# Column sums of V's weights moved from TensorE to DMA transposes and VectorE, V of four blocks from raw rows, and first loads in pairs

## The chip, the cores and the metric

The kernel runs on one core of a Trainium2 chip. The metric is the device time of one execution in microseconds, as the median of several runs. The kernel before took 237.02 us, the median of three runs from 236.8 to 237.28.

TensorE multiplies matrices and writes to PSUM, VectorE and ScalarE do element-wise work and copy PSUM to SBUF, GpSimd (POOL) does small work and issues some transfers, and SyncE (SP) issues most transfers. They run side by side and wait for each other through semaphores.

## The reference

The input x has 2048 rows of 512 numbers in bf16. Each row is layer-normalized once (`xn`). Two branches read `xn`, and their outputs are added to x:

```python
qkv = xn @ wqkv                       # 512 -> 3 x 512: 32 heads of 16
logits = q[s] . k[s - 2*w] * scale    # w = 0..7: eight rows back, two apart
o = sum_w softmax(logits)[w] * v[s - 2*w]
A = o @ wo                            # 512 -> 512

z = gelu(xn @ w_in)                   # 512 -> 1792, split into z1 and z2 of 896
g = w_sp @ layernorm(z2) + b_sp       # w_sp is 2048 x 2048, over the rows
B = (z1 * g) @ w_out                  # 896 -> 512
out = x + A + B
```

What matters here is V, the third part of `qkv`. Since the normalization is a subtraction and a scale per row, V can also be had from the raw rows: `v = rstd * (x @ wv) - rstd * mean * colsum(wv)`, where `colsum(wv)` is the sum of each of wv's 512 columns.

## The kernel before

The rows are cut into 16 blocks of 128. Every operation is recorded as a task with a name, an engine, an estimated duration, a priority, and the buffers that it reads and writes (`Plan.add`). A list scheduler (`Plan.schedule`) then simulates the engines with these estimates and fixes the order of tasks on each engine and the PSUM bank of each result; PSUM has eight banks of 512 fp32 columns, and some tasks need a pair. At run time each engine follows its list strictly and waits where a semaphore has not come. Besides, some orders are written out by hand (lines 1003 to 1015): for TensorE's first tasks, for VectorE's and ScalarE's first tasks. The table `land` (line 1018) tells the scheduler when the first loads are expected.

The stages in order of time:

- **Start.** TensorE runs eight matmuls on constants (`warm`, line 560) while the first loads come. ScalarE's queue issues blocks 0 and 1 of x, SP's queue the two halves of wv (256 KB each), block 2, the two halves of w_in's z2 part (448 KB each), blocks 3 to 7 one by one (128 KB each), Q's and K's weights, and blocks 8 to 15.
- **Layer norm** (`ln_block`): VectorE computes mean and variance (`bnst`, `bnag`, lines 599 and 601), POOL the power to -1/2 (`rstd`, line 611), VectorE the normalized block (`norm`, line 623). Blocks 0 to 3 are transposed by TensorE against an identity matrix (`xTr`, line 579) and copied to SBUF by ScalarE (`xTe`, line 587). Blocks 4 to 15 are transposed by DMA on SP's queue (`xTd`, line 617).
- **V of blocks 0 and 1** doesn't wait for the norm. The raw block is transposed (`xTx`, line 579) and copied (`xTc`, line 606), and V is computed from it (line 654). The column sums of wv come from TensorE, by four matmuls with a matrix of ones (`cs`, line 638); ScalarE copies them, negated, to `ncs` (line 642); VectorE adds mean times column sum in PSUM (`fix`, line 660); ScalarE scales by rstd, writes V in the order (d, h) (`Ve`, line 663), and POOL's queue stores it to `vscr` in DRAM (`Vw`, line 668). V of blocks 2 to 15 is computed from the normalized block.
- **z2** (`z2_block`, lines 766 to 779): 8 matmuls of 448 columns per block into a pair of banks, then GELU with row sums on ScalarE (`z2g`) and a square with row sums (`z2s`).
- **Q and K** (`qk_pair`, line 677) for waves of four blocks, into pairs of banks; VectorE forms the products for eight offsets (lines 698 and 703), TensorE reduces them over heads (`red`, line 713), and the softmax follows on VectorE and ScalarE (lines 728 to 752).
- **z1** (line 812), then the mixing over rows `g` (line 907), the longest stage, with w_sp transposed by DMA (line 880). Beside it VectorE multiplies the attention with V read back from DRAM (`ldVs`, `pv`, lines 930 to 941), and a DMA transposes the result (`OTd`, line 944).
- **Output** (lines 963 and 972): 11 matmuls per block, a final addition of x on VectorE (`fin`, line 978), and a store.

The lines of the hand-written order for TensorE and ScalarE that lie around the change:

```python
["xTx0", "cs_0", "V0_0", "xTx1", "cs_1", "V0_1", "xTr0", "V1_0", "xTr1", "V1_1",
 "z2_0_0", "z2_0_0b", "z2_0_1", "xTr2", "z2_1_0", "z2_1_1", "V2_0", "V2_1", "xTr3", "z2_2_0"]
("xTc0_0", "xTc0_1", "xTc1_0", "xTc1_1", "xTe0_0", "xTe0_2", "cse", "xTe1_0", "xTe2_0", "z2g0",
 "Ve0", "xTe3_0", "z2g1", "Ve1", "Ve2", "z2s0")
```

Of the kernel before, what the change touches and what calls it, by code (L numbers as in the profile page):

```python
# [36 lines left out]
class Plan:  # L37
# [85 lines left out]
    def schedule(self, dma_bw=300.0, xbar_bw=190.0, dma_lat=1300.0, dma_pre=400.0, issue=None, tol=40.0, land=None,  # L123
# [49 lines left out]
        while left:  # L173
            pick = None
            for e in ENGS:
                sc = []
                for t in cand[e]:
                    r = max(t.ready, free[e])
                    for b in t.banks:
                        if b.base is None:  # L180
                            p = place(b)
                            if p is None:
                                r = None
                                break
                            r = max(r, p[2])
# [31 lines left out]
            if t.dma is not None:  # L217
                iss = issue[e]
                t.eng_end = r + iss
# [4 lines left out]
                t.end = xe + dma_lat  # L224
# [114 lines left out]
def build_kernel(nc, A_x, A_wqkv, A_wo, B_x, B_w_in, B_w_sp, B_b_sp, B_w_out, out, report=False, emit=True):  # L339
# [12 lines left out]
    NWARM = 8  # L352
# [3 lines left out]
    vscr = nc.dram_tensor("vscr", (16 + S, 512), BF).ap()  # L356


    off = {}
# [11 lines left out]
    place(3584, w_in1=0, tg=0, On=2048, xcT=0, ncs=1024)  # L371
# [8 lines left out]
    off["xn"] = off["attn"]  # L380
    AR = top[0]
# [4 lines left out]
    for name, n in (("prime", 4), ("mx", 128), ("Zb", 256), ("Z", 128), ("maskt", 128), ("st6", NB * 6),  # L386
                    ("mv", NB * 2), ("vpe", NB), ("rstd", NB), ("s1", NB), ("s2", NB), ("m2", NB), ("msq", NB),
# [8 lines left out]
    with ExitStack() as es:  # L396
# [59 lines left out]
        for s_ in range(2):  # L456
            R1(("wv", s_), "wv", 1024, 1024 * s_)
# [8 lines left out]
        for hf in range(2):  # L466
            for b in range(2):
                R1(("xcT", b, hf), "xcT", 256, 512 * b + 256 * hf)
            R(("xnT", 0, hf), "sb", [(off["xnT"] + dc * S, off["xnT"] + dc * S + 128) for dc in (2 * hf, 2 * hf + 1)])
        R1("ncs", "ncs", 1024)  # L470
# [20 lines left out]
        def dma(eng, fn, nbytes, chan, reads=(), writes=(), name="", xbar=False, prio=0.0, after=()):  # L491
            return T(eng, fn, reads=reads, writes=writes, name=name, prio=prio, after=after,
                     dma=dict(chan=chan, nbytes=nbytes, xbar=xbar))
# [7 lines left out]
        ncs = A("ncs", 1024).bitcast(F32)  # L501
# [15 lines left out]
        def ld_wv(hf):  # L517
            dma("sp", lambda e: e.dma_start(AC(off["wv"] + 1024 * hf, [[512, 2], [1, 512]]),  # L518
                                            A_wqkv[256 * hf:256 * hf + 256, 1024:1536].rearrange("(c p) n -> p c n",
                                                                                               p=128)),  # L520
                256 * 512 * 2, ("wv", hf), writes=[("wv", hf)], name="ldwv%d" % hf)
# [13 lines left out]
        def ld_wqk(which, eng):  # L535
# [5 lines left out]
        dma("act", lambda e: e.dma_start(A("xin", 512), x2[0:128, :]), 128 * 512 * 2, ("xin", 0),  # L541
            writes=[("xin0", 0), ("xin0", 1)], name="ldx0")
        ld_x(1, "act")
        ld_wv(0)
        ld_wv(1)
        ld_x(2, "sp")
        ld_win2a()
        ld_win2b()
        ld_x(3, "sp")
        ld_x(4, "sp")  # L550
        ld_x(5, "sp")
        ld_x(6, "sp")
        ld_x(7, "sp")
# [19 lines left out]
        def pe_tr(src, keys, name):  # L573
# [8 lines left out]
            T("pe", tr, reads=keys + ["ident"], writes=[bk], est=(430.0 if name == "xTx0" else 4 * c_mm(128)), name=name)  # L582
# [10 lines left out]
        def ln_block(b):  # L593
# [9 lines left out]
            if b < 2:  # L603
                bc = pe_tr(xin, xk, "xTx%d" % b)
                for hf in range(2):
                    T("act", (lambda hf: lambda a: a.activation(A("xcT", 256, 512 * b + 256 * hf), P(bc, 256, 256 * hf),
                                                                ACTF.Copy))(hf),
                      reads=[bc], writes=[("xcT", b, hf)], est=c_act(256), name="xTc%d_%d" % (b, hf), prio=-1)
# [23 lines left out]
        def colsum():  # L632
            bk = plan.bank("cs")
            for hf in range(2):
                def mm(t, hf=hf):
                    last = None
                    for dc in (2 * hf, 2 * hf + 1):
                        last = t.matmul(P(bk, 512), ones[:, 0:128], A("wv", 512, 512 * dc), start=(dc == 0),
                                        stop=(dc == 3))
                    return last  # L640
                T("pe", mm, reads=[("wv", hf)], writes=[bk], est=2 * c_mm(512) * (1 if hf else 2), name="cs_%d" % hf, prio=2)
            T("act", lambda a: a.activation(ncs, P(bk, 512), ACTF.Copy, scale=-1.0), reads=[bk],  # L642
# [427 lines left out]
```

## Time and profile before

| | |
|---|---|
| median of three runs | 237.02 us |
| span of the profiled execution | 236.1 us |
| TensorE busy | 231.7 us (98%) |
| VectorE busy | 207.4 us (88%) |
| ScalarE busy | 96.5 us (41%) |
| moved by DMA | 43.86 MB, 186 GB/s over the span |

The profile is of one execution. Its span runs from the first to the last instruction, and the measured time holds some 0.9 us more around it. Times in the timeline are counted from the start of the span. PE is TensorE, PEld its weight loads, DVE VectorE, ACT ScalarE, SPq, ACTq and POOLq the queues of the engines that issue transfers. A line of the timeline gives start, length, engine, source line, operation, output and inputs, the count of instructions merged, and in brackets how long the engine had been idle and what ended that. Some matmul records are missing from the trace, so counts of matmuls in it are a little low.

### The profile page before, as it was taken

To read this page: it belongs to the slowest core of one execution; us is meant where nothing else is said; L and a number is where in the kernel's file an instruction comes from. 1 tells how busy PE (TensorE), PEld (TensorE's weight loads), DVE (VectorE), ACT (ScalarE), POOL (GpSimd) and SP (SyncE) were. 2 spreads that over 40 slices of the span, in tenths; PEclk is the share of its full clock that TensorE was granted. 3 is DMA by queue.
4 is the path that set the end of the run, shared out by engine and by line. 5 is a ranking of instruction groups with operands and counts; after the bars stand their busy time and mean duration, and the time that the engine had idled before them with its cause. 6 is when DMAs were issued, how large, how long until landed. Compare 5 with 4: busy or idle time off the path is not lost.

```text
span 236.1 us, 2974 instructions
## 1 busy us (share of the span) xinstructions
PE 231.7 (98%) x1114; PEld 109.1 (46%) x1135; DVE 207.4 (88%) x269; ACT 96.5 (41%) x145; POOL 32.7 (14%) x56
## 2 busy tenths in 40 slices
PE   8999999999999999999999999999999999999996
PEld 3455555555444444444444444444444444444443
DVE  3799899999998899999699998986989997999432
ACT  3598889888967895510120531111111111000000
POOL 2259650311733100000000000000000000000000
PEclk9999999999999999999999999999999999999999
DMA  7998969991048325430999999998995959936432
GB/s 211 352 283 163 243 146 217 195 202 44 22 165 260 92 85 69 104 118 0 226 347 252 225 266 180 200 304 187 346 258 175 261 161 303 193 95 181 135 96 69
DMA packets 82013, 43.86 MB, mean 186 GB/s; under 512 B 54336, under 2 KB 81360, under 8 KB 82000
## 3 DMA queue, kind: packets, MB, share of 16 engines
q1 hardware_dynamic: 80768, 41.27, 71.5%
q0 software_dynamic: 800, 2.11, 2.8%
q10 hardware_dynamic: 432, 0.30, 0.6%
q8 instruction: 9, 0.15, 0.3%
q14 instruction: 4, 0.03, 0.1%
HBM read 26.35 MB, written 4.21 MB: 129 GB/s over the span
## 4 chain that ended last, share of the span: by engine, by line
PE 94%; DMA 3%; SPq 1%; ACT 1%; issue 1%; DVE 0%
PE ps L907 41%; PE ps L677 12%; PE ps L972 10%; PE ps L812 10%; PE ps L766 9%; PE ps L963 6%; PE ps L654 5%; DMA arena<-in_B_w_in_dram 3%; PE ps L713 1%; ACT arena L774 0%; SPq L518 0%; ACT arena L587 0%; PE ps L579 0%; SPq L514 0%; SPq L524 0%
## 5 line engine op out<-in xcount | busy, mean ns | idle before, releaser
L907 PE MATMUL ps<-arena 128*128 128x512 bf16 x439 | 96.6, 379 | 0.5
L907 PEld LDWEIGHTS ps<-arena 128*128 128x128 bf16 x448 | 43.7, 98 | 53.1 <-issue 0.4
L915 ACT ACTIVATE arena<-ps 128x1024 bf16<-128x1024 f32 (+1 forms) x16 | 14.7, 917 | 78.0 <-PE ps L907 78.0
L698 DVE TENSOR_TENSOR arena<-arena 128x4096 bf16<-128x4096 bf16 x16 | 36.5, 2282 | 0.1
L935 DVE TENSOR_TENSOR arena<-arena 128x4096 bf16<-128x4096 bf16 x16 | 36.4, 2283 | 0.0
L938 DVE TENSOR_TENSOR arena<-arena 128x2048 bf16<-128x2048 bf16 (+1 forms) x32 | 29.9, 948 | 0.0
L677 PE MATMUL ps<-arena 128*128 128x512 bf16 x126 | 28.7, 379 | 0.1
L703 DVE TENSOR_TENSOR arena<-arena 128x4096 bf16<-128x4096 bf16 x12 | 27.4, 2287 | 0.1
L972 PE MATMUL ps<-arena 128*128 128x512 bf16 (+2 forms) x117 | 26.9, 366 | 0.1
L766 PE MATMUL ps<-arena 128*128 128x448 bf16 x128 | 26.0, 352 | 0.5 <-DMA arena<-in_B_w_in_dram 0.5
L812 PE MATMUL ps<-arena 128*128 128x512 bf16 x110 | 24.4, 379 | 0.1
L978 DVE TENSOR_TENSOR arena<-ps,arena 128x512 bf16<-128x512 f32 (+2 forms) x17 | 11.2, 658 | 11.7 <-PE ps L972 11.7
L677 PEld LDWEIGHTS ps<-arena 128*128 128x128 bf16 x128 | 14.5, 113 | 13.0
L766 PEld LDWEIGHTS ps<-arena 128*128 128x128 bf16 x128 | 12.3, 98 | 12.7 <-ACT arena L642 0.7
L686 ACT ACTIVATE arena<-ps 128x1024 bf16<-128x1024 f32 x16 | 16.3, 1021 | 4.4 <-PE ps L677 4.1
L972 PEld LDWEIGHTS ps<-arena 128*128 128x128 bf16 x119 | 11.4, 98 | 12.8
L812 PEld LDWEIGHTS ps<-arena 128*128 128x128 bf16 x112 | 10.9, 98 | 13.2 <-ACT arena L818 0.3
L963 PE MATMUL ps<-arena 128*128 128x512 bf16 (+2 forms) x66 | 16.5, 366 | 0.1
L774 ACT ACTIVATE arena<-ps 128x896 bf16<-128x896 f32 x16 | 14.6, 914 | 3.2 <-PE ps L766 3.1
L818 ACT ACTIVATE arena<-ps 128x1024 bf16<-128x1024 f32 (+1 forms) x16 | 13.9, 923 | 4.9 <-PE ps L812 4.8
L654 PE MATMUL ps<-arena 128*128 128x512 bf16 x60 | 15.6, 379 | 0.2
L779 ACT ACTIVATE arena<-arena 128x896 bf16<-128x896 bf16 x16 | 15.1, 945 | 0.0
(61 smaller groups left out, 168.5 us busy)
## 6 DMA issues: line engine op xcount, KB each, us to landing
arena<-vscr SPq DMA_DIRECT2D x16, 1024.0 KB, 7.1
arena<-in_A_x_dram SPq DMA_DIRECT2D x30, 128.0 KB, 3.6
vscr<-arena POOLq DMA_DIRECT2D x16, 128.0 KB, 3.0
out_dram<-arena SPq DMA_DIRECT2D x15, 128.0 KB, 1.8
arena<-in_A_wqkv_dram SPq DMA_DIRECT2D x2, 512.0 KB, 6.9
arena<-in_B_w_in_dram SPq DMA_DIRECT2D x2, 448.0 KB, 6.1
arena<-in_B_w_in_dram SPq DMA_DIRECT2D x1, 896.0 KB, 5.9
arena<-in_B_w_out_dram SPq DMA_DIRECT2D x1, 896.0 KB, 4.9
```

The costliest lines, as they stand in the source:

```text
L654: last = t.matmul(P(bk, 512), A("xcT", 128, 512 * b + 128 * dc) if b < 2 else xTv(b, dc), A("wv", 512, 512 * dc), start=(dc == 0), stop=(d ...
L677: last = t.matmul(P(bk, 512, 512 * which), AC(off["wqk"] + 2048 * which + 512 * dc + c, [[4, 128]]), AC(off["xnT"] + dc * S + 512 * j, [[1 ...
L686: T("act", lambda a: a.activation(AC(qo, [[ko - qo, 2], [1, 512]]), P(bk, 1024).rearrange("p (t n) -> p t n", t=2), ACTF.Copy, scale=0.5), ...
L698: T("dve", (lambda pbv, qb, kb: lambda v: v.tensor_tensor(pbv, qb, kb, ALU.mult))(pbv, qb, kb), reads=rd, writes=[("pb", s_)], est=c_tt(40 ...
L703: T("dve", (lambda av, bv: lambda v: v.tensor_tensor(av, av, bv, ALU.add))(av, bv), reads=[("pb", 1)], writes=[("pb", acc)], est=c_tt(4096 ...
L766: last = t.matmul(P(bk, 448, 512 * hf), xTv(b, dc), AC(off["w_in2"] + 896 * dc + 448 * hf, [[1, 448]]), start=(dc == 0), stop=(dc == 3))
L812: last = t.matmul(P(bk, 512, 512 * i), AC(off["w_in1"] + 896 * dc + 128 * fc, [[1, 128]]), AC(off["xnT"] + dc * S + 512 * j, [[1, 512]]), ...
L907: last = t.matmul(P(bk, 512, 512 * i), AC(off["z2"] + FH * sh + 128 * fc, [[1, 128]]), AC(off["wT%d" % r_] + sh * 512, [[1, 512]]), start= ...
L935: T("dve", lambda v: v.tensor_tensor(tv, tv, av, ALU.mult), reads=[("attn", b)], writes=[("Vs", sv)], est=c_tt(4096), name="pv%d" % b, pri ...
L938: T("dve", (lambda n: lambda v: v.tensor_tensor(A("Vs", n, 4096 * sv), A("Vs", n, 4096 * sv), A("Vs", n, 4096 * sv + n), ALU.add))(n), wri ...
L963: last = t.matmul(P(bk, cn), AC(off["OT"] + 512 * tb + 128 * cc, [[1, 128]]), AC(off["wo"] + 512 * cc + c0, [[1, cn]]), start=(cc == 0), s ...
L972: last = t.matmul(P(bk, cn), AC(off["z1T"] + fc * S + 128 * tb, [[1, 128]]), AC(off["w_out"] + 512 * fc + c0, [[1, cn]]), start=False, sto ...
```

## The change

1. **Column sums.** TensorE's four matmuls, ScalarE's copy and the buffer `ncs` go. Four DMA transposes on SP's queue (`wvT`) turn wv so that its columns lie along partitions; they are ordered after the transposes of blocks 4 to 11. One reduction on VectorE (`csum`) sums 2048 elements per partition to 4. The 512 sums are stored to DRAM by a transfer on POOL's queue (`csw`) and read back, broadcast to all partitions, by another (`csr`) into `csb`.
2. **V of blocks 0 to 3 from raw rows** (`NRAW = 4`). ScalarE copies each V out of PSUM with the factor rstd into an fp32 buffer (`vraw`); after the column sums are there, VectorE adds -mean * rstd (`mr`, one small operation for the four blocks) times column sum and writes V in the order (d, h) (`fix`). The store `Vw` follows. Blocks 2 and 3 get a raw transpose `xTx` and a copy `xTc`, and keep the normalized transpose, which z2, Q, K and z1 read. V's first matmuls are cut into finer tasks.
3. **Loads.** Block 0 comes as two halves of 64 partitions on SP's and ScalarE's queues. Blocks 2 and 3, 4 and 5, 6 and 7 come in pairs of 256 KB. The warm-up has seven matmuls.
4. **Orders and estimates.** The hand-written orders put V of blocks 0 to 3 ahead of z2; in ScalarE's order `xTe3` stands ahead of `z2g0`. The scheduler gets other estimates for DMA transposes and landings, and places two pairs of banks for one task at once. The buffers for raw transposes, `vraw`, `csb` and `wvT` lie in z1's area.

In the new fixed order, VectorE's column sum stands between its first and second wave-0 products, its four fixes ahead of wave 1's first product sum, and TensorE's first reduction `red0` behind z2 of block 15 and the first half of V of block 13.

```diff
+        for h, q_ in enumerate(("sp", "act")):
+            dma(q_, (lambda h: lambda e: e.dma_start(ar[64 * h:64 * h + 64, off["xin"]:off["xin"] + 512],
+                                                     x2[64 * h:64 * h + 64, :]))(h),
+                64 * 512 * 2, ("xin0", h), writes=[("xin0", h)], name="ldx0%s" % "ab"[h])
         ld_x(1, "act")
-        ld_wv(0)
-        ld_wv(1)
-        ld_x(2, "sp")
+        for d0, dn in ((0, 2), (2, 2)):
+            ld_wv(d0, dn)
+        ld_x2(2)
         ld_win2a()
         ld_win2b()
-        ld_x(3, "sp")
-        ld_x(4, "sp")
-        ld_x(5, "sp")
-        ld_x(6, "sp")
-        ld_x(7, "sp")
+        ld_x2(4)
+        ld_x2(6)
...
         def colsum():
-            bk = plan.bank("cs")
-            for hf in range(2):
-                def mm(t, hf=hf):
...
-                        last = t.matmul(P(bk, 512), ones[:, 0:128], A("wv", 512, 512 * dc), start=(dc == 0),
-                                        stop=(dc == 3))
...
-            T("act", lambda a: a.activation(ncs, P(bk, 512), ACTF.Copy, scale=-1.0), reads=[bk],
-              writes=["ncs"], est=c_act(512), name="cse", prio=-0.5)
+            for dc in range(4):
+                dma("sp", (lambda dc: lambda e: e.dma_start_transpose(AC(off["wvT"] + 128 * dc, [[512, 4], [1, 128]]),
+                                                                      A("wv", 512, 512 * dc)))(dc),
+                    128 * 512 * 2, ("wvT", dc), reads=[("wv", dc)], writes=[("wvT", dc)], name="wvT%d" % dc, xbar=True,
+                    prio=0.5, after=lnd[4:12])
+            T("dve", lambda v: v.tensor_reduce(Fv("cs", 4), AC(off["wvT"], [[512, 4], [1, 512]]), AX.X, ALU.add),
+              reads=[("wvT", dc) for dc in range(4)], writes=["cs"], est=2290, name="csum", prio=4.5)
+            dma("pool", lambda e: e.dma_start(bass.AP(tensor=cscr.tensor, offset=cscr.offset, ap=[[4, 128], [1, 4]]),
+                                              Fv("cs", 4)),
+                2048, "cswr", reads=["cs"], writes=["cscr"], name="csw", prio=1)
+            dma("pool", lambda e: e.dma_start(csb, bass.AP(tensor=cscr.tensor, offset=cscr.offset, ap=[[0, 128], [1, 512]])),
+                128 * 2048, "csrd", reads=["cscr"], writes=["csb"], name="csr", prio=1)
...
-            if b < 2:
-                T("dve", lambda v: v.scalar_tensor_tensor(P(bk, 512), ncs, Fv("mv", 1, 2 * b), P(bk, 512),
-                                                          ALU.mult, ALU.add),
-                  reads=["ncs", ("mv", b)], writes=[bk], est=690, name="fix%d" % b, prio=1)
...
+            if b < NRAW:
+                T("act", lambda a: a.activation(vraw(b), P(bk, 512), ACTF.Copy, scale=Fv("rstd", 1, b)),
+                  reads=[bk, ("rstd", b)], writes=[("vraw", b)], est=c_act(512), name="Ve%d" % b, prio=4)
+                T("dve", lambda v: v.scalar_tensor_tensor(
+                    vdh.rearrange("p d (c h) -> p d c h", c=4), csb.rearrange("p (h d c) -> p d c h", d=16, c=4), Fv("mr", 1, b),
+                    vraw(b).rearrange("p (c h d) -> p d c h", d=16, c=4), ALU.mult, ALU.add),
+                  reads=["csb", "mr", ("vraw", b)], writes=[("Vn", sl)], est=690, name="fix%d" % b, prio=6)
...
-                      ["xTx0", "cs_0", "V0_0", "xTx1", "cs_1", "V0_1", "xTr0", "V1_0", "xTr1", "V1_1",
-                       "z2_0_0", "z2_0_0b", "z2_0_1", "xTr2", "z2_1_0", "z2_1_1", "V2_0", "V2_1", "xTr3", "z2_2_0"],
+                      ["xTx0", "xTx1", "V0_0", "V0_1", "V1_0", "V1_1", "V0_2", "xTx2", "V0_3", "V1_2", "V1_3", "xTx3", "V2_0", "V2_2",
+                       "xTr0", "V3_0", "V3_2", "xTr1", "z2_0_0", "z2_0_0b", "z2_0_1", "xTr2", "z2_1_0", "z2_1_1", "xTr3", "z2_2_0"],
...
-                      ("xTc0_0", "xTc0_1", "xTc1_0", "xTc1_1", "xTe0_0", "xTe0_2", "cse", "xTe1_0", "xTe2_0", "z2g0",
-                       "Ve0", "xTe3_0", "z2g1", "Ve1", "Ve2", "z2s0"), ("V10_1", "Q3_3")):
+                      ("xTc0_0", "xTc0_1", "xTc1_0", "xTc1_1", "xTc2_0", "xTc3_0", "xTe0_0", "xTe0_2", "Ve0", "xTe1_0", "Ve1", "xTe2_0", "Ve2",
+                       "xTe3_0", "z2g0", "Ve3", "z2g1", "z2s0"), ("V10_2", "Q3_3")):
```

## The prediction

> **What bounds the kernel now.** I read the page's busy shares first, then the timeline of the first 22 us, the chain of work that ended last, and the landings of the first loads.
>
> ```profile
> span 236.1 us, 2974 instructions
> PE 231.7 (98%) x1114; PEld 109.1 (46%) x1135; DVE 207.4 (88%) x269; ACT 96.5 (41%) x145; POOL 32.7 (14%) x56
> ...
> PE 94%; DMA 3%; SPq 1%; ACT 1%; issue 1%; DVE 0%
> ```
>
> TensorE is on the chain for 94% of the span. The DMA share is one piece at the start, as the chain shows (start, length, what):
>
> ```profile
> 2.79 6.50 DMA arena<-in_B_w_in_dram
> 9.34 0.93 PE ps L766 x4
> ...
> 14.61 0.86 PE ps L654 x4
> 15.47 6.47 PE ps L677 x30
> ```
>
> The timeline puts the same stretch beside ScalarE:
>
> ```profile
> 0.84 2.93 PE L560 MATMUL ps<-const-bfloat16-1.0 128*128 128x512 bf16 x8 [0.84 <-PEq L1055]
> 3.73 0.61 PE L579 MATMUL ps<-arena 128*128 128x128 bf16 x4
> 4.26 0.85 PE L638 MATMUL ps<-arena,const-bfloat16-1.0 128*128 128x512 bf16 x2
> 4.38 0.66 ACT L606 ACTIVATE arena<-ps 128x256 bf16<-128x256 f32 x2 [1.14 <-PE ps L579]
> 4.95 0.60 PE L654 MATMUL ps<-arena 128*128 128x512 bf16 x2
> 8.22 0.92 PE L766 MATMUL ps<-arena 128*128 128x448 bf16 x4 [0.28 <-DMA arena<-in_B_w_in_dram]
> 9.34 0.93 PE L766 MATMUL ps<-arena 128*128 128x448 bf16 x4 [0.21 <-DMA arena<-in_B_w_in_dram]
> 12.71 0.39 PE L579 MATMUL ps<-arena 128*128 128x128 bf16 x4
> 13.13 0.60 ACT L587 ACTIVATE arena<-ps 128x512 bf16<-128x512 f32 x1 [0.53 <-PE ps L579]
> 13.63 0.91 ACT L774 ACTIVATE arena<-ps 128x896 bf16<-128x896 f32 x1
> 14.43 0.20 ACT L774 ACTIVATION_READ_ACCUMULATOR arena<-ps 128x1 f32 x1
> 15.31 6.64 PE L677 MATMUL ps<-arena 128*128 128x512 bf16 x30
> ```
>
> From 15.31, the first Q/K matmul, TensorE runs on to 234.2; the waits list none of its matmuls in that stretch. A 512-column matmul advances it by 0.216 us (the chain's 10.74 us for about 50 of them), a 448-column one by 0.189 (3.03 for 16), four 128-column ones by 0.22. Both versions have done the same work when Q/K starts, except for the column sum and two transposes. So **time after = time before − (15.31 − new start of Q/K) + any new wait behind it**, and I need only these two numbers. The profiled span of 236.1 lies 0.9 under the median of 237.02; I put differences on the median.
>
> **Before Q/K: the budget.** Between 3.73 and 15.31 TensorE does 4 column-sum, 16 V, 6 transpose groups (each like one 512 matmul) and 24 z2 matmuls: 26 × 0.216 + 24 × 0.189 = 10.15 us in 11.58. So 1.43 us is idle time or a slow clock (L638's two took 0.43 each, as in the warm-up; from 4.95 on the full rate shows). The change takes away 4 × 0.216 = 0.86 and adds the raw transposes of blocks 2 and 3, 0.43. The new floor is 3.51 + 24 × 0.216 + 24 × 0.189 = 13.2.
>
> **Where it will really start.** Step by step:
>
> 1. Warm-up: one 128-column matmul less, so it ends at 3.51 (2.93 less 0.107, from 0.84, with its tail) instead of 3.77. x0 landed at 3.7 (0.80 + 2.9). It now comes as two halves at the head of two queues, no longer beside a 256 KB weight load. Bounds 3.2 to 3.7; I take 3.55, so xTx0 starts there. *Against this:* the Trainium skill, "DMA: Bandwidth & Descriptors", Rules for kernel authors, says that two transfers to disjoint partition halves serialize on the same 16 engines and gain nothing; by it x0 lands at 3.7 again and the sum below would end at 236.65 instead of 236.5. No run here separates the two so far.
> 2. xTx0 to the first copied half took 0.65 (3.73 to 4.38), from there to the first V matmul 0.57. V0 starts at 4.77. wv's first half, now second on SP, lands between 4.2 (as before) and 4.65 (one issue of 0.45 later); not later than the copy.
> 3. V0_0, V0_1, V1_0, V1_1, V0_2 follow. The first pays 0.43, the others 0.216: 6.06 with no gap. x1 landed at 4.55, its transpose and copies let V1 start at 5.4 to 5.6, so up to 0.2 more. wv's second half landed at 5.3, in time. Then xTx2 needs the pair of blocks 2 and 3. Block 2 alone landed at 5.7; 131 KB more at the 350 GB/s of this stretch is 0.37, so 6.05. I take xTx2 at 6.15 (bounds 5.8 to 6.7, the upper if the pair is skewed as w_in's halves are).
> 4. From xTx2 to z2: 11 V matmuls and 4 transpose groups, 15 × 0.216 = 3.24, so z2 at 9.4.
> 5. The loads of w_in's second half have one more 128 KB ahead of them. They landed at 8.1 and 9.3 and were what TensorE waited for (0.28 and 0.21). Plus 0.37: 8.5 and 9.7, wanted at 9.4 and 10.15. This wait goes; what is late next is the V work put ahead of it.
> 6. z2 of blocks 0 to 2 and two transposes: 24 × 0.189 + 0.43 = 4.97, to 14.37.
> 7. A new wait: Q/K needs two banks, and ScalarE's written order puts the GELU of z2 block 0 (z2g0) behind xTe3, the copy of the last transpose. The rows for such a sequence: transposes start 12.71, GELU and its read-out end 14.63, 1.92 us, and 0.06 to be seen. TensorE has 0.22 + 1.51 to do meanwhile, so it idles 0.25. Q/K starts at 14.62.
>
> That is 0.69 earlier. Bounds: xTx2 at 5.8 gives 14.27 (1.04 earlier), at 6.7 gives 15.17 (0.14).
>
> **Behind Q/K: what moves and what covers it.**
>
> - SP: ten issues ahead of Q's and K's weights become eight, so these are not later than 12.7 and 14.2 where they landed. Four transposes of wv (1.27 us each on SP, from 10.48 for 8) go between the eighth and ninth xn transposes: 5.1 us, so blocks 12 to 15, issued by 31.2 before, land about 37 instead of 33.5; their first use, z2 of block 12, is at 49.2. The w_sp transposes behind them end by 56 instead of 50.9 and are wanted at 98.2.
> - VectorE: the column sum is 2048 elements in one reduce; L728's 1024 took 1.21, so 2.2 to 2.4. Fixes go from two to four, 0.75 each by L660; small `mr` 0.15. In all 2.3 + 1.5 + 0.15 = 3.95 us more, and the two early fixes (9.0 and 10.8) leave, so norms of blocks 4 to 7 come some 1.5 us sooner, which Q/K of wave 1 needs if it is to start 0.7 earlier.
> - The first logits reduction (L713, 64.64; VectorE had finished at 63.2) is the first place where TensorE meets that extra work. By the new order TensorE does z2 of block 15, V10 to V12, half of V13 and a Q/K pair ahead of it: about 6.25 us, so 64.64 + 6.25 − 0.69 = 70.2. VectorE does 2.3 + 3.0 + 0.15 and four z2 normalizations (1.8) more, and starts its products 1.5 to 2 earlier: 68.5 to 69. It holds by about 1.4 us.
> - Tail: the last transpose of the attention output is issued at 219.5, lands 3.3 later, and is wanted at 231.6. That is 8.8 us of slack against 3.95. VectorE's own idle time shows it, too:
>
> ```profile
> DVE arena L978 <- PE ps L972: 11.7, 10, 1.7
> ```
>
> - Column sums go out and come back by two transfers on POOL. Its 128 KB writes landed in 2.0 to 3.9 us, so twice that from 32 is 40; the fixes stand at about 53 in VectorE's order. Behind the first transfer on POOL stands the z2 power (3.05 us, L795), whose result VectorE uses 4.6 us later: covered by 0.8. V stores of blocks 0 to 3 move from 13.5-18.8 to after 54; V is read back from 97.7 on.
> - Output blocks: TensorE may wait once or twice for a bank behind VectorE's later final adds (0.69 each). Bounds 0 to 0.7; I take 0.15, since the final adds lag by up to 2.8 us now and eight banks hold 17 us of it.
>
> Sum: 237.02 − 0.69 + 0.15 = 236.5.
>
> **Rivals.**
>
> - *Cover that was there anyway* (B): the pair of x lands at 6.5 to 7, or ScalarE's longer queue (two copies of 0.6 more, the column sum's 0.6 less) delays a V copy. Q/K starts at 15.0 to 15.5: 236.7 to 237.2. For it: w_in's half took 2.4 us after x2 for its 459 KB, far under 350 GB/s. Against: each x row is a 1 KB piece, and x2 followed wv by 0.4.
> - *Slower: the clock rises late* (C). The full rate began at 4.95, after 4.1 us of nearly unbroken matmuls. The new order leaves TensorE idle around 3.95 to 4.77. If the rate then rises one stretch of that length later, matmuls from 4.95 cost double for some 3.4 us, 1.7 us lost less 0.2 of gaps: Q/K at 16.1, so 0.8 lost, and with the 0.15 for the output blocks 238.0. It decides if a V matmul after 6.0 still takes 0.43. The Trainium skill, "TensorE: Matmul & The Clock Gate", Part 1, states that an activity window of about 3.4 us, free-running, must be busy before the half rate is lifted, and gives no share that counts as busy. The rows agree with the half rate at first; the granted clock in the profile reads 1.00 throughout and doesn't show it.
> - *Slower: VectorE arrives late at the first reduction* (D). Its fixes now read 4-byte operands in a scattered order from SBUF. From 1.1 us each, or if the column sums return after 55, the 1.4 us of cover are gone and TensorE waits one for one. At 1.5 us each: 3.0 − 1.4 = 1.6 lost, 238.1. Against it: L730 reads PSUM scattered at 1.2 us for 1024, no dearer per element.
> - *More than forecast* (E): no waits at all, near the floor: 235.3 to 235.9.
>
> **How the numbers follow.** Forecast (A), Q/K at 14.3 to 15.0 and nothing lost behind: 236.0 to 236.7, 0.55. B 0.20, C 0.10, D 0.12, E 0.03. The likeliest gives 236.5. For 8 in 10 the range drops E, half of C and half of D: 235.9 to 238.0. A difference under 0.2% (0.47 us, 236.55 to 237.49) is about what can't be told from none: of A about 0.4 lies below 236.55 and 0.15 above, B gives 0.03 faster, 0.14 same, 0.03 slower, E is faster, C and D slower. That is 0.46, 0.29, 0.25.
>
> **What would show it.** Right: xTx2 at 6.0 to 6.3, z2's first matmul at 9.3 to 9.6 with no wait on w_in, Q/K's first at 14.6 behind a short wait for ScalarE L774, no TensorE wait over 0.1 us before the output blocks, VectorE's reduce 2.2 to 2.4, fixes near 0.75. Wrong: V matmuls of 0.43 past 6 us (C); a wait ahead of the 32-row reduction near 70 (D); xTx2 at 6.6 or later (B).

## The result, and the profile after

| | before | after |
|---|---|---|
| median | 236.91 us (6 runs, 236.78 to 237.37) | 238.99 us (6 runs, 237.81 to 239.72) |
| ratio after / before | | 1.0077, 95% interval 1.0056 to 1.0098 |
| span of the profiled execution | 236.1 us | 237.1 us |
| first Q/K matmul | 15.31 | 15.44 |
| from there to the end of the last matmul | 218.87 | 219.48 |
| from there to the end of the span | 1.92 | 2.18 |

The change made the kernel 2.1 us slower. It was forecast 0.5 us faster, and 238.99 lies above the range (235.9 to 238.0). The profiled execution took 238.31, so it is one of the quicker ones of the changed kernel. Its time exceeds its span by 1.2, and in the other executions below the two differ by 1.2 to 1.6; the prediction's 0.9 set the span of one execution against the median of others.

The busy times and the chain of the page, after:

```profile
span 237.1 us, 3018 instructions
PE 232.3 (98%) x1138; PEld 109.1 (46%) x1138; DVE 211.6 (89%) x273; ACT 96.9 (41%) x146; POOL 31.9 (13%) x58
...
PE 67%; DVE 22%; DMA 4%; SPq 3%; POOL 1%; issue 1%; DVEq 0%
```

TensorE fell from 94% of the chain to 67%, and VectorE holds 22% where it had none: somewhere TensorE now waits for VectorE. The timeline of the start shows another loss ahead of that (start, length, engine, line, operation, count; in brackets the idle time and what ended it):

```profile
0.80 0.59 SPq L566 DMA_DIRECT2D arena<-in_A_x_dram  x1
0.81 0.57 ACTq L566 DMA_DIRECT2D arena<-in_A_x_dram  x1
1.43 0.85 ACTq L534 DMA_DIRECT2D arena<-in_A_x_dram  x1
1.44 1.08 SPq L543 DMA_DIRECT2D arena<-in_A_wqkv_dram  x2
3.46 0.63 PE L602 MATMUL ps<-arena 128*128 128x128 bf16 x4
5.33 0.40 PE L602 MATMUL ps<-arena 128*128 128x128 bf16 x4 [1.24 <-DMA arena<-in_A_x_dram]
5.57 1.46 PE L692 MATMUL ps<-arena 128*128 128x512 bf16 x5
6.86 0.39 PE L602 MATMUL ps<-arena 128*128 128x128 bf16 x4
10.13 1.68 PE L806 MATMUL ps<-arena 128*128 128x448 bf16 x8
15.44 4.91 PE L717 MATMUL ps<-arena 128*128 128x512 bf16 x22 [0.16 <-ACT arena L814]
```

Block 0 did land early: its transpose starts at 3.46. Then TensorE stands still for 1.24 us, until block 1 lands at 5.33; it had landed at 4.55 before. From 5.33 on nothing holds it for longer than the 0.16 shown: 4.80 us from `xTx1` to z2 at 10.13, 5.3 more to Q/K.

The second loss is at the first logits reduction:

```profile
32.21 2.29 DVE L662 TENSOR_REDUCE fpool<-arena 128x4 f32<-128x2048 bf16 x1 [1.02 <-DMA arena<-arena]
54.06 4.19 DVE L701 SCALAR_TENSOR_TENSOR arena<-arena,fpool 128x512 bf16<-128x512 f32 x4
69.07 2.28 DVE L743 TENSOR_TENSOR arena<-arena 128x4096 bf16<-128x4096 bf16 x1
70.51 0.59 PE L692 MATMUL ps<-arena 128*128 128x512 bf16 x2
71.40 1.05 PE L753 MATMUL ps<-arena 128*32 128x512 bf16 x16 [0.29 <-DVE arena L743]
```

and in the waits of TensorE's weight loads (engine, line, what it waited for: us in total, times, longest):

```profile
PEld ps L753 <- DVE arena L743: 0.8, 1, 0.8
PEld ps L852 <- DVE arena L770: 0.6, 1, 0.6
```

The four fixes took 4.19 us instead of the 3.0 assumed. VectorE had also waited 1.02 for the transposes of wv. It finishes the sum that the reduction reads at 71.35 (69.07 + 2.28), after TensorE is ready for it. The 0.61 us that the stretch behind Q/K is longer lies here, by my estimate about 0.4 ahead of the reduction and 0.2 at the bank behind it (line 770).

So in this execution the span is 1.0 longer: 0.13 by Q/K, 0.61 behind it, and 0.26 after the last matmul. Against the forecast of 14.62, Q/K is 0.82 late. The rest of the median's 2.1 us had to be found in other executions; none at the median itself was profiled.

### The profile page after: what moved, and what is told of

It is laid out like the page before. It is cut to its first block, busy times and chain, and to the rows that moved or that the text cites. A ratio compares the mean times of both kernels' runs of the same rounds, so it can differ in the third digit from the quotient of the medians.

```text
span 237.1 us, 3018 instructions
## 1 busy us (share of the span) xinstructions
PE 232.3 (98%) x1138; PEld 109.1 (46%) x1138; DVE 211.6 (89%) x273; ACT 96.9 (41%) x146; POOL 31.9 (13%) x58
## 4 chain that ended last, share of the span: by engine, by line
PE 67%; DVE 22%; DMA 4%; SPq 3%; POOL 1%; issue 1%; DVEq 0%
PE ps L948 41%; PE ps L1013 10%; PE ps L852 10%; DVE arena L738 7%; PE ps L1004 6%; DVE arena L743 6%; DMA arena<-in_A_x_dram 3%; DVE arena L838 2%; SPq L658 2%; DVE arena L701 2%; DVE fpool L622 1%; DMA arena<-arena 1%; DVE arena L647 1%; DVE fpool L662 1%; POOL fpool L635 1%
## 5 line engine op out<-in xcount | busy, mean ns | idle before, releaser
L959 DVE TENSOR_TENSOR arena<-arena 128x1024 bf16<-128x1024 bf16 (+1 forms) x16 | 10.0, 625 | 5.8 <-ACT arena L956 5.8
```

## The experiments

Three explanations compete. **Loads:** the split of block 0 makes what is issued behind it late. **Clock:** TensorE's half rate lasts longer, or comes back, because TensorE is idle near 4 to 5 us. **VectorE:** the dear fixes make the first reduction late. Each run was timed beside runs of the kernel before on the same chip. "Behind Q/K" is the time from the first Q/K matmul to the end of the last matmul: 218.87 in both profiles of the kernel before.

### The changed kernel again

> The changed kernel once more, for the spread of its runs (237.8 to 239.7 so far) and a second profile. Theory F (VectorE's fixes at 1.1 us instead of 0.75 bring it late to the first logits reduction): Q/K again at about 15.4, a TensorE wait of 0.3 to 1.5 us ahead of the 32-row reduction near 71, and 0.2 to 0.6 for a bank behind it; the slow runs differ from the fast ones there. Rival S (the start): the profile shows the first transposes of x later or earlier by what the run is longer or shorter, with the wait at the reduction unchanged. Rival C (clock): V matmuls of 0.43 us past 6 us in a longer run.

Measured: 239.01 us (6 runs, 238.65 to 239.36), 1.0084 [1.0067, 1.0101]. The profiled execution took 238.65: Q/K at 16.02, 219.13 behind it.

```profile
5.32 1.04 PE L692 MATMUL ps<-arena 128*128 128x512 bf16 x4 [1.04 <-DMA arena<-in_A_wqkv_dram]
6.57 0.39 PE L692 MATMUL ps<-arena 128*128 128x512 bf16 x1 [0.20 <-DMA arena<-in_A_wqkv_dram]
7.22 0.40 PE L602 MATMUL ps<-arena 128*128 128x128 bf16 x4 [0.26 <-DMA arena<-in_A_x_dram]
```

This time block 1 was early and wv's first half late (issued at 1.44, landed at 5.24, against 4.2 before). The loss is the same in kind: what stands behind the halves of block 0 is late, on one queue or the other. Where ScalarE's queue took 0.85 us to issue block 1, as in the first profile, block 1 was late; here that issue took 0.59, SP's of wv's first half 0.82, and wv was late. The pair of blocks 2 and 3 is late here as well (7.2).

### Fixes that read in stored order

```diff
-                    vdh.rearrange("p d (c h) -> p d c h", c=4), csb.rearrange("p (h d c) -> p d c h", d=16, c=4), Fv("mr", 1, b),
-                    vraw(b).rearrange("p (c h d) -> p d c h", d=16, c=4), ALU.mult, ALU.add),
+                    vn, csb, Fv("mr", 1, b), vraw(b), ALU.mult, ALU.add),
```

> The four fixes read the scaled V and the column sums in stored order and write in stored order, all else the same, instruction for instruction; V of blocks 0 to 3 comes out in the wrong order of columns. Theory F: the fixes fall from 1.11 to about 0.7 us, VectorE is 1.6 us earlier at the first reduction, TensorE waits there no more, and the median falls by 0.7 to 1.5 us against the changed kernel. Rival S: fixes may be shorter, the median moves by under 0.3 us. If the scattered order isn't what costs, the fixes stay at 1.1.

This kernel leaves V of blocks 0 to 3 in the wrong order of columns. Measured: 239.38 us (6 runs, 237.60 to 240.23), 1.0094 [1.0063, 1.0124]. A fix took 746 ns. The groups by shape (busy us, mean ns of one | idle before), first of the changed kernel's second profile, then of this one:

```profile
L701 DVE SCALAR_TENSOR_TENSOR arena<-arena,fpool 128x512 bf16<-128x512 f32 x4 | 4.2, 1122 | 0.0
```

```profile
L701 DVE SCALAR_TENSOR_TENSOR arena<-arena,fpool 128x512 bf16<-128x512 f32 x4 | 2.7, 746 | 0.0
```

So the scattered order is what makes a fix dear. The wait at the reduction is gone and the stretch behind Q/K is back at 218.66, but this doesn't show that the cheap fixes removed it: TensorE itself came to the reduction 1.8 us later (73.21 instead of 71.40). VectorE was ready at 71.16; with dear fixes, some 1.5 us more, it would by that estimate still have been in time. The median didn't fall by the 0.7 to 1.5 that theory F asked for; the larger loss lies before Q/K, which began at 17.83 in this execution, the slowest of the six:

```profile
3.46 0.63 PE L602 MATMUL ps<-arena 128*128 128x128 bf16 x4
5.74 0.61 PE L602 MATMUL ps<-arena 128*128 128x128 bf16 x4 [1.65 <-DMA arena<-in_A_x_dram]
6.14 2.34 PE L692 MATMUL ps<-arena 128*128 128x512 bf16 x5
8.27 0.63 PE L602 MATMUL ps<-arena 128*128 128x128 bf16 x4
8.70 1.37 PE L692 MATMUL ps<-arena 128*128 128x512 bf16 x3
9.91 0.39 PE L602 MATMUL ps<-arena 128*128 128x128 bf16 x4
```

Block 1 landed at 5.73. After 1.65 us without work, the next matmuls run at half rate: five V take 2.34 instead of 1.46, a transpose group 0.63 instead of 0.39, until after 9 us. From `xTx1` to Q/K it is 12.09 us against 10.11 in the first profile, so the half rate costs about 2.0 us here. This is the clock's part, and here it follows on the loads' part. (The profile's granted clock reads 1.00 throughout this stretch; the rate is read from the lengths of the matmuls.)

### The scheduler told what a fix costs

```diff
-                  reads=["csb", "mr", ("vraw", b)], writes=[("Vn", sl)], est=690, name="fix%d" % b, prio=6)
+                  reads=["csb", "mr", ("vraw", b)], writes=[("Vn", sl)], est=1060, name="fix%d" % b, prio=6)
```

> Only the scheduler's estimate of a fix goes from 690 to 1060 ns, so that it places the first reduction and what follows by the true cost (behind both halves of V of blocks 13 and 14). The work is the same. Theory F: the wait ahead of the first reduction falls under 0.2 us and the median falls by 0.5 to 1.2 us against the changed kernel, though VectorE does as much as before. If VectorE's extra work itself were the bound, the median would stay within 0.2.

Measured: 238.9 us (9 runs, 237.43 to 240.16), 1.0073 [1.0041, 1.0104]. The median stays. Behind Q/K it is 218.65: with an honest estimate the planner puts four more matmuls of z2 and six of V (about 2.05 us) ahead of the reduction, and VectorE is ready 1.84 us before it, although each fix costs as much. Q/K began at 18.28 in the profiled execution, the slowest of the nine. TensorE waited 2.19 us for block 1, ran at the full rate from 6.28, and fell back to the half rate by 8 us; from `xTx1` to Q/K it is 12.00 us, 1.9 more than in the first profile. In the windows (stretch, busy us and count of PE, PEld, DVE, ACT, POOL, granted clock, DMA share, GB/s) the granted clock itself shows it:

```profile
8.00:9.00 1.00, 1.00 (x6) 0.58 (x5) 0.93 (x5) 0.18 (x1) 0.34 (x2) 0.50 1.06 354
9.00:10.00 1.00, 1.00 (x5) 0.44 (x4) 0.93 (x5) 0.42 (x1) 0.41 (x1) 0.50 1.07 367
...
11.00:12.00 1.00, 1.00 (x9) 0.61 (x8) 0.97 (x3) 0.27 (x2) 0.00 (x0) 1.00 1.10 375
```

It reads 0.50 from 8 to 10 us and 1.00 from 11 on.

### Block 0 whole again

```diff
-        for h, q_ in enumerate(("sp", "act")):
-            dma(q_, (lambda h: lambda e: e.dma_start(ar[64 * h:64 * h + 64, off["xin"]:off["xin"] + 512],
-                                                     x2[64 * h:64 * h + 64, :]))(h),
-                64 * 512 * 2, ("xin0", h), writes=[("xin0", h)], name="ldx0%s" % "ab"[h])
+        dma("act", lambda e: e.dma_start(A("xin", 512), x2[0:128, :]), 128 * 512 * 2, ("xin", 0),
+            writes=[("xin0", 0), ("xin0", 1)], name="ldx0")
```

> Block 0 of x is loaded as one transfer on ScalarE's queue again, with wv's first half first on SP's; all else the same. Rival S: block 1 lands near 4.6 instead of 5.3, its transpose and with it z2 and Q/K start 0.3 to 0.7 us earlier, and the median falls by as much. Theory F: Q/K may start earlier, but TensorE then waits that much longer at the first reduction, which VectorE sets; the median moves by under 0.3.

Measured: 237.14 us (12 runs, 236.65 to 238.56), 1.0009 [0.9993, 1.0025], against 239.01 for the changed kernel in the same series. This one part of the change costs 1.9 us, more than either theory forecast. All else of the change is in this kernel, and its profiled execution (236.85) goes by the prediction's steps:

```profile
3.54 0.61 PE L600 MATMUL ps<-arena 128*128 128x128 bf16 x4
4.41 0.61 PE L600 MATMUL ps<-arena 128*128 128x128 bf16 x4 [0.26 <-DMA arena<-in_A_x_dram]
...
6.15 0.39 PE L600 MATMUL ps<-arena 128*128 128x128 bf16 x4
...
9.42 1.68 PE L804 MATMUL ps<-arena 128*128 128x448 bf16 x8
...
14.89 1.46 PE L715 MATMUL ps<-arena 128*128 128x512 bf16 x6 [0.32 <-ACT arena L812]
```

Block 1 landed at 4.4. `xTx2` is at 6.15 and z2 at 9.42, as forecast; the wait for w_in is gone. Q/K is at 14.89 behind a wait of 0.32 for ScalarE. Behind Q/K it is 218.83: with the same dear fixes a weight load waits 0.42 for VectorE ahead of the reduction, but no matmul does, since VectorE too is about a microsecond earlier (its wave 0 products start at 23.38 instead of 24.32). What seems to count is how far VectorE starts these products behind TensorE's Q/K. With dear fixes and the old estimate, the three profiles that lose time there have 8.54 to 8.95 us, this one 8.49. So VectorE's loss depends on the loads' loss.

### Block 0 whole, and fixes in stored order

ScalarE writes the scaled V in the order (d, h), and one more transfer on POOL's queue brings the column sums into that order in DRAM, so that a fix reads and writes without jumps.

```diff
+            dma("pool", lambda e: e.dma_start(
+                bass.AP(tensor=cscp.tensor, offset=cscp.offset, ap=[[32, 16], [8, 4], [1, 8]]),
+                bass.AP(tensor=cscr.tensor, offset=cscr.offset, ap=[[4, 16], [1, 4], [64, 8]]), allow_slow_non_contiguous=True),
+                2048, "cspm", reads=["cscr"], writes=["cscp"], name="csp", prio=1)
...
-                T("act", lambda a: a.activation(vraw(b), P(bk, 512), ACTF.Copy, scale=Fv("rstd", 1, b)),
+                T("act", lambda a: a.activation(vraw(b).rearrange("p (d h) -> p d h", d=16),
+                                                PC(bk.col(), [[1, 16], [16, 32]]), ACTF.Copy, scale=Fv("rstd", 1, b)),
...
+                    vn, csb, Fv("mr", 1, b), vraw(b), ALU.mult, ALU.add),
```

> Block 0 whole again, and the fixes made cheap: ScalarE writes the scaled V in the order (d, h), a small extra DRAM transfer on POOL's queue puts the column sums in the same order, so the fixes read and write in stored order. Theory S+F (the split of block 0 costs the start, the scattered fixes cost the wait ahead of the first reduction): fixes 0.75 us, no TensorE wait over 0.2 us ahead of the first reduction nor behind it, Q/K at 14.9, median 0.3 to 0.6 us below the kernel with block 0 whole alone (237.14 there against 237.19 of before), so 236.6 to 236.9. If the waits behind Q/K have another cause, no change.

Measured: 237.05 us (12 runs, 236.74 to 238.58), 1.0006 [0.9990, 1.0022]; a fix took 752 ns, Q/K at 14.66, 218.95 behind it. VectorE finishes ahead of the reduction at 69.60 instead of 70.15, and the weight load's wait of 0.42 is gone. No measurable gain over block 0 whole alone: with the loads in time, the fixes' cost is hidden.

### Block 0 whole, and the scheduler told what a fix costs

The edit of the estimate above, on the kernel with block 0 whole.

> Block 0 whole, fixes as scattered as in the changed kernel but with 1060 ns as the scheduler's estimate, so the first reduction is placed later. Theory S+F: the wait ahead of the reduction falls from about 0.5 to under 0.2, median 236.6 to 236.9. If VectorE's extra work itself sets the end, it stays at 237.1.

Measured: 237.53 us (12 runs, 237.07 to 238.73), 1.0026 [1.0010, 1.0042]. Behind Q/K 218.89, so again no loss at the reduction; but the forecast gain didn't come, and the interval lies above the kernel before. In the profiled execution Q/K was at 15.25, because the first five V ran at half rate for longer:

```profile
4.48 0.61 PE L600 MATMUL ps<-arena 128*128 128x128 bf16 x4 [0.25 <-DMA arena<-in_A_x_dram]
4.88 2.03 PE L690 MATMUL ps<-arena 128*128 128x512 bf16 x5
```

They took 2.03 instead of 1.50, at the same order of work and nearly the same landings: the moment at which the full rate is granted differs between executions, and here it moves Q/K by 0.4 to 0.6 us, with the loads in time.

### The split alone, in the kernel before

```diff
-        dma("act", lambda e: e.dma_start(A("xin", 512), x2[0:128, :]), 128 * 512 * 2, ("xin", 0),
-            writes=[("xin0", 0), ("xin0", 1)], name="ldx0")
+        for h, q_ in enumerate(("sp", "act")):
+            dma(q_, (lambda h: lambda e: e.dma_start(ar[64 * h:64 * h + 64, off["xin"]:off["xin"] + 512],
+                                                     x2[64 * h:64 * h + 64, :]))(h),
+                64 * 512 * 2, ("xin0", h), writes=[("xin0", h)], name="ldx0%s" % "ab"[h])
```

> The kernel before with one edit alone: block 0 of x as two halves on SP's and ScalarE's queues. Theory S: block 1 and wv land 0.5 to 1.5 us later, Q/K starts 0.5 to 1.5 later than 15.3, and the median is 0.5 to 1.8 us above the kernel before. Rival (the split hurts only with what else the change does, the V work ahead of z2): within 0.3 of before.

Measured: 238.39 us (6 runs, 238.05 to 239.40), 1.0062 [1.0043, 1.0082]. The split costs 1.2 us with nothing else changed. Behind Q/K 218.87, exactly as in the kernel before; the whole loss is at the start (Q/K at 16.21):

```profile
0.80 0.58 SPq L542 DMA_DIRECT2D arena<-in_A_x_dram  x1
...
1.42 0.86 ACTq L514 DMA_DIRECT2D arena<-in_A_x_dram  x1
1.43 1.08 SPq L518 DMA_DIRECT2D arena<-in_A_wqkv_dram  x2
...
4.78 1.03 PE L640 MATMUL ps<-arena,const-bfloat16-1.0 128*128 128x512 bf16 x2 [0.59 <-DMA arena<-in_A_wqkv_dram]
```

The halves take SP's and ScalarE's queue 0.58 and 0.57 us to issue, against 0.42 for the whole block; wv's first half leaves at 1.43 instead of 0.80, and the column sums wait 0.59 for it.

### Block 0 whole, but first on SP

```diff
-        dma("act", lambda e: e.dma_start(A("xin", 512), x2[0:128, :]), 128 * 512 * 2, ("xin", 0),
+        dma("sp", lambda e: e.dma_start(A("xin", 512), x2[0:128, :]), 128 * 512 * 2, ("xin", 0),
```

> Block 0 whole, but as the first transfer of SP's queue, ahead of wv, and block 1 first on ScalarE's. It tells whether the halves or the place ahead of wv cost the start. If halves of 64 partitions: block 0 lands near 3.6, block 1 by 4.4, wv's first half by 4.9, and the median is within 0.3 us of the kernel with block 0 whole on ScalarE's queue. If it is the place ahead of wv: wv's halves land 0.5 us later, V starts near 5.4, and the median is 0.5 to 1.5 us above.

Measured: 237.49 us (12 runs, 237.28 to 239.88), 1.0021 [1.0003, 1.0040]. Here wv also stands second on SP, behind a whole block of 128 KB, and block 1 is first on ScalarE's queue. Both blocks land by 3.6, wv's first half at 4.3 and TensorE isn't held by it; wv's second half and the pair of blocks 2 and 3 are late (waits of 0.45 at 6.17 and 0.30 at 6.87). Standing second on SP is thus not what costs 1.2 us; this order costs 0.3 by the medians against the kernel before. In the profiled execution TensorE waited at the reduction again (219.32 behind Q/K).

### The kernel before, once more

> The kernel before once more, for a second profile of it. The profile shown of it belongs to one execution; if the start varies from execution to execution, Q/K starts up to 0.6 us earlier or later than 15.3 here and the time moves by as much, with nothing else changed.

Measured: 237.25 us (one run), Q/K at 15.25, 218.87 behind it. In this execution the first matmuls ran at half rate until about 6.6 us, and z2 began at 8.54 without a wait for w_in. In the first profile the full rate came at 4.95, z2 began at 8.22 and waited 0.49 in all for w_in. Q/K began within 0.06 of each other. In these two executions the old order's wait for w_in takes up a late rise of the rate; the new order has no such wait.

### Block 0 in two halves of columns, in the kernel before

```diff
+            dma(q_, (lambda h: lambda e: e.dma_start(ar[:, off["xin"] + 256 * h:off["xin"] + 256 * h + 256],
+                                                     x2[0:128, 256 * h:256 * h + 256]))(h),
```

> The kernel before with block 0 of x in two halves on SP's and ScalarE's queues, but halves of the columns (128 partitions of 512 B) instead of halves of the partitions (64 of 1 KB). If 64 partitions are what makes the start late (the issue of 0.58 us and the later landings): the issue takes 0.40 to 0.45 again and the median stays within 0.4 us of before. If it is the two queues at once, or the small transfer ahead of wv: 0.8 to 1.4 above before, as with halves of the partitions (1.2 above).

Measured: 238.14 us (7 runs, 237.62 to 239.22), 1.0055 [1.0034, 1.0076]. Halves with all 128 partitions issue in 0.40 us, yet cost 1.1 us too:

```profile
0.80 0.40 SPq L542 DMA_DIRECT2D arena<-in_A_x_dram  x1
...
5.00 1.03 PE L640 MATMUL ps<-arena,const-bfloat16-1.0 128*128 128x512 bf16 x2 [0.80 <-DMA arena<-in_A_wqkv_dram]
```

So neither the 64 partitions nor the dearer issue is needed for the loss. Here, too, the half rate follows on the late load: it lasts until about 8.4 us, so the loads' part and the clock's part aren't separate in this number. What the two splits share is that only 128 KB are under way until the second pair of issues. The windows of 2.5 to 3.5 us (last column GB/s) show the traffic: first the kernel before, then the changed kernel, then the halves of columns, then the whole block first on SP:

```profile
2.50:3.00 0.50, 0.50 (x3) 0.22 (x2) 0.00 (x0) 0.50 (x1) 0.00 (x0) 1.00 0.88 266
3.00:3.50 0.50, 0.50 (x4) 0.22 (x2) 0.00 (x0) 0.23 (x2) 0.00 (x0) 1.00 1.09 381
```

```profile
2.50:3.00 0.50, 0.50 (x3) 0.22 (x2) 0.00 (x0) 0.50 (x1) 0.00 (x0) 1.00 1.20 191
3.00:3.50 0.50, 0.50 (x4) 0.22 (x3) 0.19 (x1) 0.50 (x1) 0.00 (x0) 1.00 0.60 139
```

```profile
2.50:3.00 0.50, 0.50 (x3) 0.23 (x2) 0.00 (x0) 0.50 (x1) 0.00 (x0) 1.00 0.41 71
3.00:3.50 0.50, 0.50 (x4) 0.23 (x3) 0.40 (x1) 0.21 (x2) 0.00 (x0) 1.00 0.72 231
```

```profile
2.50:3.00 0.50, 0.50 (x3) 0.22 (x2) 0.00 (x0) 0.23 (x2) 0.00 (x0) 1.00 1.09 348
3.00:3.50 0.50, 0.50 (x4) 0.14 (x3) 0.08 (x1) 0.00 (x0) 0.00 (x0) 1.00 0.98 332
```

With 64 KB at the head of each queue the traffic drops to 139 or 71 GB/s where the others move 266 to 381. From 2.0 to 4.0 us (half-microsecond windows, each GB/s times 0.5) the kernel before moves 550 KB, the changed kernel 392, the column halves 466, the whole block on SP 553. That the small first issues leave the DMA engines short of work is argued from these windows; no run separates it further.

### The changed kernel with work in the gap

```diff
+        bf = plan.bank("fill")
+        for wi, n_ in enumerate((512, 512, 512, 512)):
+            T("pe", (lambda n_: lambda t: t.matmul(P(bf, n_), ones[:, 0:128], ones[:, 0:n_], start=True,
+                                                   stop=True))(n_),
+              writes=[bf], est=1.0, name="fill%d" % wi, prio=1000)
...
-                      ["xTx0", "xTx1", "V0_0", "V0_1", "V1_0", "V1_1", "V0_2", "xTx2", "V0_3", "V1_2", "V1_3", "xTx3", "V2_0", "V2_2",
+                      ["xTx0", "fill0", "fill1", "fill2", "fill3", "xTx1", "V0_0", "V0_1", "V1_0", "V1_1", "V0_2", "xTx2", "V0_3", "V1_2", "V1_3", "xTx3", "V2_0", "V2_2",
```

> The changed kernel with four 512-column matmuls on constants between the transposes of block 0 and of block 1, where TensorE was idle for 1.2 to 2.2 us; results go to a bank nobody reads. Theory C (the idle time lets the rate stay or fall to half, on top of the late landing): no V matmul of 0.43 us past 6.5, the runs over 239.4 go, and the median falls by 0.3 to 1.0 us against 239.0. If the late landing is all, the median stays within 0.2 or rises.

Measured: 238.06 us (9 runs, 237.65 to 239.37), 1.0051 [1.0032, 1.0070]. The four matmuls on constants take TensorE from 3.89 to 5.60 and compute nothing that is used:

```profile
3.89 1.91 PE L589 MATMUL ps<-const-bfloat16-1.0 128*128 128x512 bf16 x4
5.60 0.63 PE L608 MATMUL ps<-arena 128*128 128x128 bf16 x4
6.02 1.50 PE L698 MATMUL ps<-arena 128*128 128x512 bf16 x5
...
15.93 4.29 PE L723 MATMUL ps<-arena 128*128 128x512 bf16 x19
```

Added work, but 0.9 us less in the median than the changed kernel (238.99 and 239.01), as theory C forecast; by the ratios to the kernel before, it is 0.6 to 0.8. The interval overlaps with that of the first series and just touches that of the second, so the size is rough. Nor does the profiled execution (237.94) show where the gain lies: Q/K at 15.93 is within 15.44 and 16.02 of the changed kernel's two profiles, and 218.89 behind it shows that the loss at the reduction, 0.3 to 0.6 us there, is gone (VectorE's products start 7.68 us behind Q/K). So a part of the gain may be VectorE's. That the filler spares half rates as long as the two above fits the times (239.37 at most, against 239.72) but wasn't profiled.

### Fixes in stored order, block 0 whole, and some filler

The kernel with block 0 whole and fixes in stored order, with two filler matmuls of 512 and 128 columns behind `xTx0`.

> The version with block 0 whole and fixes in stored order (237.05 against 237.18 of before, two of twelve runs at 238.4 and 238.6), with one 512- and one 128-column matmul on constants between the transposes of blocks 0 and 1. Theory C: the runs near 238.5 go and the full rate stands by 5.0 us; median 236.5 to 237.0, at or under before. If the filling only delays the second transpose: 237.1 to 237.4.

Measured: 237.23 us (12 runs, 236.83 to 237.84), 1.0009 [0.9998, 1.0019]. The longer executions of the version without filler (238.36 and 238.58) don't appear in these twelve, which may be chance, and the median isn't lower: theory C's forecast missed. In its profiled execution (237.76) Q/K began at 15.69, about a microsecond later than in that version's. It was not the filler's own time that held TensorE: behind the filler it waited 0.45 us for block 1, which landed at 5.26 instead of 4.56, and then began at half rate. None of the versions beats the kernel before beyond its interval.

## Why the prediction was wrong

**Formula: held.** In the eleven profiled executions in which no matmul waits for VectorE at the first reduction or at the bank behind it, the stretch behind Q/K is 218.65 to 218.95, before and after the change alike. Only in the three where one waits is it longer (219.13, 219.32, 219.48). Q/K's start was the number to get right.

**Step 1, block 0's landing: right, and beside the point.** Its halves landed by 3.2, its transpose began at 3.46 against a forecast of 3.55. The Trainium skill, "DMA: Bandwidth & Descriptors", Rules for kernel authors, advises against two transfers to disjoint partition halves because they serialize. Here the block did land a little earlier (3.2 against 3.7 and 3.5 in the two profiles of before). The advice not to split was right all the same, for a cost of 1.2 us in what follows, which the Trainium skill doesn't state there.

**Steps 2 and 3: the ones that failed.** Step 2 allowed wv's first half one issue of 0.45 more, to 4.65 at most; step 3 took block 1's landing from the kernel before, 4.55. Nothing had changed in block 1's own line, so I moved it by nothing. It landed at 5.33, 5.73 and 6.23 in three profiles of the split start, and where it was early, wv's first half came at 5.24. That is 0.6 to 1.7 us, on the path. In the first profile Q/K was late by as much as block 1 (0.82 and 0.78); in the others it was later by more (1.4 to 3.7), where the pair of blocks 2 and 3 or the rate came on top. The split alone, in the kernel before, costs 1.2 us of the 2.1. Block 0 whole in the changed kernel brings back 1.9, since with late loads the new order also pays at the reduction (0.3 to 0.6) and, in some executions, with the rate (1.9 to 2.0); how much each has in the median was not separated.

**Rival B, chance 0.20: its signs came, not its price.** `xTx2` began at 6.86 and Q/K at 15.44, as it had said (6.6 or later, 15.0 to 15.5), but in the first profile because of block 1; in the second the pair, landed at 7.2, held TensorE for 0.26. With block 0 whole the pair landed at 6.02 (forecast 6.05).

**Rival C, chance 0.10: it took part, mostly behind the late loads.** I tied it to the gap of 0.8 us that the new order leaves by itself. With block 0 whole it shows in one of three profiles (Q/K 0.4 to 0.6 later). Its price of 1.7 us shows only where late loads widen the gap to 1.65 and 2.19 us: there the half rate lasts to beyond 9 us, or returns by 8, and costs 1.9 to 2.0. Filler in the gap took 0.6 to 0.9 us off the median, of which the rate's share is open. The Trainium skill, "TensorE: Matmul & The Clock Gate", Part 1, speaks of a free-running activity window of about 3.4 us and of run-to-run variation from it. The half rate that ends at about 5 and at 6.6 us in two executions of the kernel before fits a free-running window. No run here shows the window itself, and here gaps of 1.65 to 2.2 us were followed by half rate.

**Rival D, chance 0.12: its mechanism is there, at a part of the price.** A fix in the scattered order took 1.12 us, just past the 1.1 that I named as the point where it decides; 746 ns in stored order. The row that I set against it, a multiplication that reads PSUM (line 730), didn't show it. VectorE was done at 71.35 instead of 68.5 to 69: the four fixes took 1.2 more than the 3.0 of my sum, and the wait of 1.02 for the transposes of wv wasn't in it. TensorE lost 0.3 to 0.6 us instead of 1.6, and only where VectorE had itself begun about a microsecond later than with block 0 whole on ScalarE's queue. That the dear fixes are needed for this loss is argued from these sums; no run has cheap fixes with VectorE as late as in the changed kernel and TensorE on time.

**Steps 4 to 7: right.** With block 0 whole: `xTx2` 6.15, z2 9.42 (forecast 9.4), no wait for w_in, a wait of 0.32 for ScalarE (forecast 0.25), Q/K at 14.66 and 14.89 (forecast 14.62) in two of the three profiles, 15.25 in the third. The column sum took 2.29 (forecast 2.2 to 2.4). The slack of 8.8 us at the last transposes covered VectorE's extra work: behind 77 us no profile shows a matmul waiting for VectorE.

**The expected gain itself.** Even with block 0 whole the median equals that of the kernel before, though two of the three profiled executions show Q/K 0.4 to 0.6 earlier and take 236.74 and 236.85. These are among the quickest of their twelve. The times of these kernels spread further up (to 238.6 and 238.7) than those of the kernel before (237.81 at most in all series). I read this so: the old order waits for w_in, so a late rise of the rate costs it nothing, while the new order pays for it in full. The kernel before at half rate until 6.6 with Q/K still at 15.25 supports this, and so does the third profile with block 0 whole, whose longer half rate put Q/K at 15.25; a whole distribution of starts was not recorded, so it stays argued.

## What to carry to other kernels

When a load at the head of a queue is changed, move every load behind it on every queue: re-derive the landing of each transfer that the first matmuls need, and don't keep a landing from the old trace because its own line is unchanged. In this kernel it was right to start with large transfers: splitting the first one brought its own data 0.3 to 0.5 us sooner and cost the kernel before 1.2 us. Before taking a wait away, ask what variation it absorbs; and bound an element-wise operation by a row with the same memory, type and access order.

## What the runs showed of the hardware that was not expected

- Two first transfers of 64 KB, one on each of two queues, in place of one of 128 KB beside one of 256 KB: traffic of 392 or 466 KB from 2.0 to 4.0 us instead of 550, for halves by partitions and by columns.
- Issuing a transfer to 64 partitions took 0.58 us, one of the same bytes to 128 partitions 0.40. Behind two halves of 64 partitions the next issue took longer on one of the two queues: on ScalarE's 0.84 to 0.86 instead of 0.46 in four profiles, on SP's 0.82 in two.
- The granted clock read 0.50 from 8 to 10 us, behind a gap of 2.19 us that had ended at 6.28.
- VectorE's operation on two fp32 operands of 128 x 512 in SBUF took 1.12 us in a scattered order and 0.75 in stored order.
- Reordering 2 KB in DRAM by 4-byte pieces kept POOL's queue waiting for 11.8 us:

```profile
48.88 0.56 POOL L670 DMA_DIRECT2D arena<-cscp  x1 [11.79 <-DMA cscp<-cscr]
```
